# First x turned by TensorE instead of by DMA, w2 loaded earlier, later gelu' of one chunk and a rearranged end in a convolution-and-joint kernel with its gradients

## The chip, the cores and the metric

The kernel runs on one core of a Trainium2 chip. The metric is the time of one execution on the device in microseconds (us); "before" is the median of three runs. A core has TensorE (PE, with its weight loads PEld), VectorE (DVE), ScalarE (ACT), GpSimd (POOL) and SyncE (SP), each with its own queue of instructions in a fixed order. SP here only issues DMA transfers.

## What is computed

A small speech model's forward pass and all of its gradients. x has 2 x 16000 rows of 256 numbers (bfloat16), g has 2 x 8 rows.

```python
h  = gelu(conv3(x, w1))[:, ::2]            # 3 taps, 256x256 each; every second row is kept
f  = gelu(conv3(h, w2))[:, ::2]            # now 2 x 4000 rows
fe = f @ w_f ; ge = g @ w_g
j  = tanh(fe[:, :, None] + ge[:, None])    # 2 x 4000 x 8 x 256
out = j @ w_o
# outputs: out, and the gradients of x, w1, w2, g, w_f, w_g, w_o for a given grad_out
```

## The kernel before

**Chunks.** The 8000 kept positions are cut into 17 chunks: the first has 2 blocks of 128 positions, fifteen have 4 blocks (512 positions), the last has one block of 64. A position needs 4 rows of x. Per chunk there are three stages:

- `stage_a`: XC, the chunk's x with features on the partitions, goes through `conv1` twice (the rows of odd place "o", then those of even place "e"), each followed by `conv_gelu`; then `conv2` and the product with WF, which gives FE. `conv_gelu` (L433 to L490) has per half of the features a Square and a Gelu on ACT (L464, L466) and a product on DVE (L468), then, for the gradient, a tanh on ACT (L476) and five DVE operations (L478 to L486) that write G1o, G1e or G2 ("gelu'"). Its scratch tiles are g_sq (class gsq, three buffers) and g_s (class gs, two buffers); each is opened by the first matmul of a convolution (L460) and held until gelu' is done.
- `stage_j`: in four pairs of the 8 rows of g. JT = tanh(FE + GE) on ACT (L637); for the first two chunks JT is turned by PE and copied to JR (L655), later JR is computed by itself (L660, L665). PE makes the output (L314, WO), the gradient of w_o in GWO, and grad_out times WOT; DVE multiplies it by JT squared (JSQ) into ZS, NGZ and NGP (L705, L720), and the last sum is GN.
- `stage_de`: the way back. GN gives GF, GH and the gradient of x (GX_SB), and with the rows HR, GNR, GHR and XR the gradients of the weights, added up in ACCF, ACC2 and ACC1 (L784) and stored from STAGE at the end (L775). GNR and GHR come by DMA transpose, in the last chunk by PE (`pe_rows`, L745). The gradient of g comes last from NGP by way of NGGE and ngb (L986, L989).

**Memory.** PSUM has seven free banks and one fixed, GWO, into which all chunks add the gradient of w_o.

**The order.** `Flow` takes every operation with its engines, a planned cost and a due time (`F.now` or `at`), and plays a list schedule in which each engine takes the earliest operation that could start, ties by due time. What comes out is the fixed order of every engine's queue. Some evictions (`evac`) may go to ACT or DVE, and the planner chooses. Among its numbers, COLD is the planned moment until which PE is taken as 1.8 times slower, and `land` is how long after its transfer a DMA is taken to arrive.

**The start.** PE runs 28 matmuls on a zeroed tile (L1026). SP turns chunk 0's x (512 KB) on the way by DMA transpose (L338), then the first half of chunk 1's x, then loads w2 (L1040), then the second half. ACT's queue loads w1, POOL's g, w_g, w_f and w_o. The transposed weights W1T, W2T, WG, WFT and WOT are made by PE and an eviction (`turn`, L1046) when the planner finds room.

**The end.** `last_w1` (L959) puts the last two chunks' terms for each tap of w1's gradient into one PSUM bank and stores it; `store` (L976) brings GWO and the others out.

Of the kernel before, what the change touches and what calls it, by code (L numbers as in the profile page):

```python
# [35 lines left out]
class Flow:  # L36
# [4 lines left out]
    TURN = {"TT": 250.0, "TL": 750.0, "SL": 900.0, "LL": 200.0, "TS": 250.0, "LS": 250.0, "SS": 400.0}  # L41
    BACKLOG = {"T": 1450.0, "L": 4500.0, "S": 4500.0}
    NEAR = 300.0
    COLD = 14000.0
    CROWD = 10000.0
    KIND = 16.0

# [162 lines left out]
def kernel(  # L210
# [148 lines left out]

    def load_xc(g_, at, apart=0.0):
        c = chunks[g_]
        XC = st[g_]["XC"] = buf("xr" if c.first else "xc", [P, 17, KT, P], BF16, "XC")
        lo, hi = (1 if c.first else 0), 4 * c.nb + 1
        cuts = ((0, 9), (9, 17)) if g_ == 1 else ((lo, hi),)
        for n_, (b0, b1) in enumerate(cuts):
            dma("SP", lambda b0=b0, b1=b1: XC[:, b0:b1, :, :c.np].rearrange("p j k n -> p (j k) n"),
                lambda b0=b0, b1=b1: dram(xf, 4 * c.q0 - 1 + b0, 4 * c.nb, b1 - b0, c.np),
                r=[], w=[(XC, ("m", n_))], bytes_=(b1 - b0) * c.np * D * 2, new=[XC] if n_ == 0 else [], transpose=True, at=at + n_ * apart,  # L370
                land=2500.0 if c.first else 4500.0)
        if c.first:
            pool_zero(lambda: XC[:, 0, :, 0:1], [], [(XC, "z")], at=at)
            pool_copy(lambda: XC[:, 0, :, 1:P], lambda: XC[:, 4 * c.nb, :, 0:P - 1], 254, [(XC, ("m", 0))], [(XC, "h")], at=at)
        elif c.mid:
            pool_zero(lambda: XC[:, 0, :, c.pb:c.pb + 1], [], [(XC, ("m", 0))], at=at)

    got_op = {}
# [54 lines left out]
    def conv_gelu(g_, jobs, rd, h_buf, pre, ho, gname, gcls, gshape, gsave, news):  # L433

        c = chunks[g_]
        nb, n_ = c.nb, c.np
        W = c.W
        G = buf(gcls, gshape, BF16, gname)
        here = gname == "G2"
        if here:  # L440
            sq, s = buf("gsq", [P, NB, KT, P], BF16, "g_sq"), G
            so, scr = 0, [sq, G]
        elif c.first:
            sq = s = buf("gs" if gname == "G1e" else "gsq", [P, NB, KT, P], BF16, "g_sq")
            so, scr = nb, [sq]
        else:
            sq = buf("gsq", [P, NB, KT, P], BF16, "g_sq")
            s = buf("gs", [P, NB, KT, P], BF16, "g_s")
            so, scr = 0, [sq, s]
        sk = lambda mt: (s, ("s", mt))  # L450
        qk = lambda mt: (sq, ("q", mt))
        both = lambda f: [f(mt) for mt in range(KT)]
        pss = [psum() for _ in range(KT)]
        parts = [(mt, h) for h in range(len(rd)) for mt in range(KT)]
        for k_, (mt, h) in enumerate(parts):
            lst, cost = jobs(mt, h)
            def mms(e, mt=mt, lst=lst):
                for o_, wt, rhs, s_, e_ in lst:
                    mm(o_(pss[mt]), wt(), rhs(), s_, e_)
            op("PE", cost, mms, r=rd[h] + [(sq, "b")], w=[(pss[mt], h)],  # L460
               new=([pss[mt]] if h == 0 else []) + (scr + news if k_ == 0 else []))
        for mt in range(KT):
            ps = pss[mt]
            op("ACT", c_act(W, True), lambda e, mt=mt, ps=ps: nc.scalar.activation(  # L464
                out=sq[:, 0:nb, mt, :n_], in_=blk(ps, c), func=ACT.Square, scale=GELU_SQRT_K), r=[ps], w=[qk(mt)])
            op("ACT", c_act(W, True), lambda e, mt=mt, ps=ps: nc.scalar.activation(  # L466
                out=h_buf[:, ho:ho + nb, mt, :n_], in_=blk(ps, c), func=ACT.Gelu_apprx_tanh), r=[ps], w=[(h_buf, (pre, mt))])
            op("DVE", c_dve(W), lambda e, mt=mt, ps=ps: nc.vector.scalar_tensor_tensor(  # L468
                out=s[:, so:so + nb, mt, :n_], in0=sq[:, 0:nb, mt, :n_], scalar=1.0, in1=blk(ps, c), op0=ALU.add, op1=ALU.mult),
               r=[qk(mt), ps], w=[sk(mt)])  # L470
        k = GELU_A / 2
        N = KT * W
        late = F.now + CW * 0.25
        go_ = 1 if gsave else 0
        full = lambda T_, o_=0: T_[:, o_:o_ + nb, :, :n_]
        op("ACT", c_act(N), lambda e: nc.scalar.activation(out=full(s, so), in_=full(s, so), func=ACT.Tanh, scale=k),  # L476
           r=both(sk), w=both(sk), at=late)
        op("DVE", c_dve(N, 0.25), lambda e: nc.vector.tensor_scalar(  # L478
            out=full(sq), in0=full(sq), scalar1=3.0 * k, scalar2=k, op0=ALU.mult, op1=ALU.add), r=both(qk), w=both(qk), at=late)
        op("DVE", c_dve(N, 0.5), lambda e: nc.vector.tensor_tensor(  # L480
            out=full(sq), in0=full(sq), in1=full(h_buf, ho), op=ALU.mult), r=both(qk) + [(h_buf, (pre, 0)), (h_buf, (pre, 1))], w=both(qk), at=late)
        op("DVE", c_dve(N, 0.25), lambda e: nc.vector.tensor_scalar(
            out=full(sq), in0=full(sq), scalar1=-0.5, scalar2=None, op0=ALU.add), r=both(qk), w=both(qk), at=late)
        op("DVE", c_dve(N, 0.25), lambda e: nc.vector.tensor_scalar(
            out=full(s, so), in0=full(s, so), scalar1=-1.0, scalar2=1.0, op0=ALU.mult, op1=ALU.add), r=both(sk), w=both(sk), at=late)
        op("DVE", c_dve(N, 0.5), lambda e: nc.vector.tensor_tensor(  # L486
            out=full(G, go_), in0=full(s, so), in1=full(sq), op=ALU.mult), r=both(sk) + both(qk), w=[(G, ("g", 0)), (G, ("g", 1))] + (both(sk) if here else []), new=[] if here else [G], at=late)
        st[g_][gname] = G
        if gsave:
            F.now = late  # L490
            halo(g_, G, "g", gname, gsave)
# [16 lines left out]
    def stage_a(g_, t0, dt):  # L508
# [9 lines left out]
        def conv1(l0):  # L518
# [9 lines left out]
                                    i == 0 and kt == 0, i == KK - 1 and kt == KT - 1))  # L528
                return lst, c_pe([m_ * n_] * 6)
            return jobs  # L530
        xm = [(XC, ("m", 0)), (XC, ("m", 1))]
        F.now = t0
        conv_gelu(g_, conv1(2), [xm[:1] + [W1], xm + [W1]] if two else [xm + [W1]], HT, "o", 1, "G1o", "g1o", [P, NB + 1, KT, P], "hg1", [HT])
        F.now = t0 + 0.05 * dt
        halo(g_, HT, "o", "HTo", "hho")
        if c.mid:
            pool_zero(lambda: HT[:, 0, :, c.pb:c.pb + 1], [], [(HT, ("o", "h"))])
        F.now = t0 + 0.12 * dt
        conv_gelu(g_, conv1(0), [xm[:1] + [W1], xm + [W1]] if two else [[XC, W1]], HT, "e", oE, "G1e", "g1e", [P, NB, KT, P], None, [])
        pad_tail(g_, HT, "o", (0, nb + 1))  # L540
        pad_tail(g_, HT, "e", (oE, oE + nb))
        F.now = t0 + 0.3 * dt
# [216 lines left out]
    def grad_rows(g_, name, cls, SRC, nblk, m):  # L759
        if chunks[g_].last:  # L760
            return pe_rows(g_, name, cls, SRC, 1, nblk, m)
        return tile_rows(g_, name, cls, SRC, nblk, lo=1, shape=[P, 2 * NB + (cls == "ghr"), D], land=8000.0)

    def stage():
        stage_n[0] += 1
# [2 lines left out]

    stage_n = [0]

    def acc_add(ACC, key, acc_ap, ps, g_, out, final):
        if final:
            t_ = stage()
            flat = lambda: t_[:, 0:512]
            op("DVE", c_dve(512), lambda e: nc.vector.scalar_tensor_tensor(  # L775
                out=flat(), in0=acc_ap().rearrange("p k d -> p (k d)"), scalar=-1.0, in1=ps[:],
                op0=ALU.mult, op1=ALU.subtract),
               r=[(ACC, key), ps], w=[t_], new=[t_])
            dma("SP", lambda: out.rearrange("(dt p) n -> p dt n", p=P),
# [177 lines left out]
        return terms  # L957

    def last_w1(i):  # L959
        ps = psum()  # L960
        two = [w1_terms(g_, i) for g_ in (LAST - 1, LAST)]
        n = [0, KT * sum(len(t_) for t_ in two)]

        def mms(e, terms):
            for d2 in range(KT):
                for lhs, rhs, _ in terms:
                    mm(ps[:, d2 * D:(d2 + 1) * D], lhs(d2), rhs(), n[0] == 0, n[0] == n[1] - 1)
                    n[0] += 1
        for k, t_ in enumerate(two):
            rd = []  # L970
            for _, _, l in t_:
                rd += [b for b in l if b not in rd]
            op("PE", c_pe([D] * (KT * len(t_))), lambda e, t_=t_: mms(e, t_), r=rd, w=[ps], new=[ps] if k == 0 else [])
        acc_add(ACC1, i, lambda: ACC1[:, i], ps, LAST, out_2[i], True)

    def store(dst, src, r, scale=None, after=()):  # L976
        t_ = stage()
# [44 lines left out]
       r=[(warm, 0)], w=[(warm, 1)])  # L1022
    wps = psum()

    def warm_up(e):
        for _ in range(28):  # L1026
            mm(wps[:, 0:2 * P], warm[:, 0, 0:P], warm[:, 0, 0:2 * P], True, True)
    op("PE", 28 * 120.0, warm_up, r=[(warm, 0)], w=[wps], new=[wps])

    def wload(q, dst, key, out, in_, at, land):  # L1030
        return dma(q, out, in_, r=[], w=[(dst, key)], bytes_=131072, at=at, land=land)

    load_xc(0, BIG)
    op("POOL", 500.0, lambda e: make_identity(nc, ident[:]), w=[ident])
    for i in range(KK):
        wload("ACT", W1, i, lambda i=i: W1[:, i], lambda i=i: w1[i].rearrange("(kt p) n -> p kt n", p=P), BIG, 4000.0)
    for b in range(B):
        dma("POOL", lambda b=b: GR8[:, b, :], lambda b=b: g[b], r=[], w=[(GR8, b)], bytes_=4096, at=BIG + 1, land=5000.0)
    load_xc(1, BIG, 60.0)
    dma("SP", lambda: W2[:].rearrange("p i k n -> p (i k) n"), lambda: w2.rearrange("i (kt p) n -> p (i kt) n", p=P),  # L1040
        r=[], w=[(W2, i) for i in range(KK)], bytes_=393216, load=True, at=BIG + 30.0, land=2500.0)
    wload("POOL", WG, 0, lambda: WG[:], lambda: w_g.rearrange("(kt p) n -> p kt n", p=P), BIG + 1, 8500.0)
    wload("POOL", WF, 0, lambda: WF[:], lambda: w_f.rearrange("(kt p) n -> p kt n", p=P), BIG + 2, 9000.0)
    wload("POOL", WO, 0, lambda: WO[:], lambda: w_o.rearrange("(kt p) n -> p kt n", p=P), BIG + 2, 9000.0)
# [49 lines left out]
    for k in range(NG + 1):  # L1094
# [22 lines left out]
            gg_out(int(k == LAST))  # L1117
        if k == LAST:
            gwg_out()
            store(out_7, lambda: GWO[:], [], after=gwo_ops)  # L1120
    F.now = 1e9
    ctx.enter_context(tc.manual_schedule())
    F.issue()
# [30 lines left out]
```

## Time and profile before

| | us |
|---|---|
| median of three runs | 783.84 (782.11 to 785.67) |
| the profiled execution | 784.01 |
| its span (first to last thing that the profile shows) | 782.1 |
| PE busy | 768.3 |
| DVE busy | 716.1 |
| ACT busy | 716.4 |
| POOL busy | 86.1 |
| first convolution on PE | starts at 8.03 |
| last matmul | ends at 778.0 |

The profile comes from one execution. Times in its views count from the span's start. A row of a timeline has its start, its length, engine, line, operation, written and read tile, shapes, the number of instructions put together, and in brackets how long the engine sat idle before it and what ended that. A row of waits has the waiting engine and line, what it waited for, the sum in us, how often, and the longest. A row of the windows table has the stretch, its length, and for each engine the busy time and the number of instructions, then PE's granted clock (1.00 is full), the DMA engines' share and GB/s. Lines of the kernel after are some 20 higher than those of before.

### The profile page before, as it was taken

The page shows a single profiled execution, that of the slowest core. Times are in us where ns is not written, and L with a number is a line of the kernel's source. Part 1 is how long each engine was busy: PE and PEld are TensorE (multiplying, and loading weights), DVE is VectorE, ACT ScalarE, POOL GpSimd, SP SyncE. Part 2 cuts the span into 40 slices and gives each one's busy share as a digit, 9 for nine tenths or more (in the row PEclk, how much of TensorE's full clock was granted, in tenths as well). Part 3 has the DMA queues.
Part 4 walks back from the last instruction along what each step waited for, and adds up shares of the span by engine and source line. Part 5 has one row for each costly group of instructions (what it writes and reads, how often), then busy time and mean ns, then how long its engine had stood idle before and what let it go on. Part 6 is the DMA issues. An engine that isn't in the chain of part 4 may idle for free.

```text
span 782.1 us, 15385 instructions
## 1 busy us (share of the span) xinstructions
PE 768.3 (98%) x5620; PEld 533.3 (68%) x5620; DVE 716.1 (92%) x1502; ACT 716.4 (92%) x1148; POOL 86.1 (11%) x225
## 2 busy tenths in 40 slices
PE   9799999999999999999999999999999999999997
PEld 7577667576676766767577675766767667677755
DVE  4979999998999999999999999989999999999874
ACT  5999999998999999999999999899999999999761
POOL 3001010201102010020100102001020110201000
PEclk9989999999999999999999999999999999999999
DMA  9999999999999999999999999999999999899672
GB/s 198 232 231 212 233 233 258 239 219 276 216 275 223 232 283 218 252 238 240 272 231 282 230 245 255 237 296 215 275 251 241 233 237 284 175 228 256 172 199 77
DMA packets 394890, 183.82 MB, mean 235 GB/s; under 512 B 320180, under 2 KB 388062, under 8 KB 392894
## 3 DMA queue, kind: packets, MB, share of 16 engines
q1 hardware_dynamic: 393758, 182.03, 100.6%
q8 instruction: 44, 0.72, 0.4%
q0 software_dynamic: 240, 0.41, 0.3%
q10 hardware_dynamic: 816, 0.39, 0.2%
q14 instruction: 32, 0.26, 0.1%
HBM read 52.47 MB, written 50.35 MB: 131 GB/s over the span
## 4 chain that ended last, share of the span: by engine, by line
PE 91%; ACT 4%; DVE 3%; DMA 2%; issue 1%; DVEq 0%; ACTq 0%
PE ps L314 76%; PE GWO L314 13%; DMA GNR<-GN 2%; PE psb L583 1%; DVE g_s L468 1%; ACT JT L637 1%; ACT JSQ L696 1%; PE psb L655 1%; ACT g_sq L464 1%; ACT HT L466 0%; DVE NGZ L705 0%; ACT JR L665 0%; DVE GH L846 0%; ACT JR L323 0%; PE psb L1055 0%
## 5 line engine op out<-in xcount | busy, mean ns | idle before, releaser
L637 ACT ACTIVATE JT<-FE,GE 128x512 bf16<-128x512 bf16 (+4 forms) x288 | 179.7, 686 | 0.3 <-DVE FE L328 0.2
L705 DVE SCALAR_TENSOR_TENSOR NGZ<-JSQ,ps 128x512 f32<-128x512 bf16 (+3 forms) x252 | 151.2, 608 | 7.2 <-PE ps L314 5.5
L314 PE MATMUL ps<-WO,JT 128*128 128x256 bf16 (+1 forms) x1008 | 151.8, 274 | 0.0
L314 PE MATMUL ps<-GOT,WOT 128*128 128x512 bf16 (+2 forms) x544 | 151.2, 364 | 0.1
L696 ACT ACTIVATE JSQ<-JT 128x1024 bf16<-128x1024 bf16 (+2 forms) x130 | 132.4, 1018 | 10.5 <-DVE NGZ L705 7.8
L314 PEld LDWEIGHTS <-JT 128*128 128x128 bf16 (+1 forms) x1008 | 98.8, 98 | 60.1
L323 ACT CAST OUT_SB<-ps 128x512 bf16<-128x512 f32 (+1 forms) x203 | 121.4, 606 | 15.2 <-PE ps L314 14.9
L314 PE MATMUL GWO<-GO_R,JR 128*128 128x256 bf16 (+1 forms) x1008 | 131.2, 273 | 0.3 <-ACT JR L323 0.3
L665 ACT ACTIVATE JR<-JR 128x1024 bf16<-128x1024 bf16 (+1 forms) x116 | 122.9, 1065 | 7.9 <-DVE JR L660 7.9
L720 DVE TENSOR_TENSOR ZS<-ZS,NGZ 128x1024 f32<-128x1024 f32 (+2 forms) x102 | 115.3, 1131 | 0.7
L314 PEld LDWEIGHTS <-JR 128*128 128x128 bf16 (+1 forms) x1008 | 98.2, 98 | 15.3 <-ACT JR L323 0.6
L314 PEld LDWEIGHTS <-W 128*128 128x128 bf16 x636 | 60.0, 98 | 60.1 <-issue 1.1
L314 PE MATMUL ps<-W1T,GH 128*128 128x256 bf16 (+2 forms) x506 | 94.2, 325 | 0.0
L314 PE MATMUL ps<-XC,W 128*128 128x512 bf16 (+2 forms) x432 | 86.5, 351 | 0.0
L314 PE MATMUL ps<-GHR,XR 128*128 128x256 bf16 (+1 forms) x756 | 85.6, 273 | 0.7 <-ACT GHR L323 0.7
L314 PEld LDWEIGHTS <-XR 128*128 128x128 bf16 (+1 forms) x756 | 73.8, 98 | 9.4 <-issue 0.8
L660 DVE TENSOR_TENSOR JR<-FER,GEB 128x1024 bf16<-128x1024 bf16 (+1 forms) x116 | 77.8, 673 | 0.0
L784 DVE TENSOR_TENSOR ACC<-ACC,ps 128x512 f32<-128x512 f32 x87 | 57.6, 679 | 16.1 <-PE ps L314 16.0
L314 PEld LDWEIGHTS <-WOT 128*128 128x128 bf16 x544 | 51.3, 99 | 29.7 <-issue 1.7
L314 PEld LDWEIGHTS <-GH 128*128 128x128 bf16 (+1 forms) x506 | 49.3, 98 | 24.6 <-issue 0.2
L325 ACT ACTIVATE GX_SB<-ps 128x512 bf16<-128x512 f32 (+1 forms) x88 | 52.5, 619 | 10.1 <-PE ps L314 9.7
L314 PE MATMUL ps<-GNR,HR 128*128 128x256 bf16 (+1 forms) x504 | 59.5, 273 | 1.3 <-DMA GNR<-GN 1.3
(130 smaller groups left out, 981.7 us busy)
## 6 DMA issues: line engine op xcount, KB each, us to landing
GO_R<-in_grad_out_dram SPq DMA_DIRECT2D x60, 512.0 KB, 5.3
out_dram<-OUT_SB SPq DMA_DIRECT2D x60, 512.0 KB, 4.8
XR<-in_x_dram SPq DMA_DIRECT2D x15, 1088.0 KB, 8.0
out_dram<-GX_SB SPq DMA_DIRECT2D x30, 512.0 KB, 3.4
out_dram<-STAGE SPq DMA_DIRECT2D x9, 128.0 KB, 3.5
GOT<-GO_R SPq DMA_TRANSPOSE x68, 6.2
GO_R<-in_grad_out_dram SPq DMA_DIRECT2D x4, 256.0 KB, 3.5
out_dram<-OUT_SB SPq DMA_DIRECT2D x4, 256.0 KB, 4.9
```

The lines of the kernel that those rows point to most:

```text
L314: nc.tensor.matmul(ps_ap, lhsT=lhsT, rhs=rhs, start=start, stop=stop)
L323: nc.scalar.copy(out=dst(), in_=src())
L325: nc.scalar.activation(out=dst(), in_=src(), func=ACT.Copy, scale=scale)
L464: op("ACT", c_act(W, True), lambda e, mt=mt, ps=ps: nc.scalar.activation(out=sq[:, 0:nb, mt, :n_], in_=blk(ps, c), func=ACT.Square, scale= ...
L468: op("DVE", c_dve(W), lambda e, mt=mt, ps=ps: nc.vector.scalar_tensor_tensor(out=s[:, so:so + nb, mt, :n_], in0=sq[:, 0:nb, mt, :n_], scal ...
L637: op("ACT", c_act((hi - lo) * nb, ptr=True), lambda e, j=j, mt=mt, lo=lo, hi=hi, b=b: nc.scalar.activation(out=cut(JT[:, j, mt, :W], lo, h ...
L660: op("DVE", c_dve(na * 2 * D, 0.5), lambda e, h=h, na=na, JR=JR: nc.vector.tensor_tensor(out=JR[:n_, 0:na], in0=S["FER"][:n_, 2 * h:2 * h ...
L665: op("ACT", c_act(na * 2 * D), lambda e, na=na, JR=JR: nc.scalar.activation(out=JR[:n_, 0:na], in_=JR[:n_, 0:na], func=ACT.Tanh), r=[JR], ...
L696: nc.scalar.activation(out=JSQ[:, :, :W], in_=JT[:, j, :, :W], func=ACT.Square)
L705: nc.vector.scalar_tensor_tensor(out=cut(Z[:, d2, :W], lo, hi), in0=cut(JSQ[:, d2, :W], lo, hi), scalar=1.0, in1=cut(ps[:, :W], lo, hi), o ...
L720: nc.vector.tensor_tensor(out=o_, in0=i0, in1=i1, op=ALU.add)
L784: op("DVE", c_dve(512), lambda e: nc.vector.tensor_tensor(out=acc_ap().rearrange("p k d -> p (k d)"), in0=acc_ap().rearrange("p k d -> p ( ...
```

## The change

Chunk 0's x comes in rows (two plain loads into XL), is turned by PE in 16 transposes, and four evictions write XC. w2 is first in SP's queue. The identity that PE's transposes need is made first on POOL. The warm-up has 20 matmuls instead of 28. The gelu' of chunk 1 is due 0.8 of a chunk after its place instead of 0.25. GNR and GHR of the chunk before the last are planned to land sooner, and the last chunks' terms of tap 0 of w1's gradient are summed in GWO's bank, after GWO has been stored, instead of in a free bank.

```diff
-    COLD = 14000.0
+    COLD = 7000.0
...
+    def rows_xc(c, XC, at):
+
+        XL = buf("out", [P, 4 * c.nb, D], BF16, "XL")
+        for h in range(2):
+            src = xf[0:8 * P, :].rearrange("(p r) d -> p r d", r=8)[:, 4 * h:4 * h + 4, :]
+            dma("SP", lambda h=h: XL[:, 4 * h:4 * h + 4, :], lambda src=src: src, r=[], w=[(XL, h)], bytes_=P * 2048,
+                new=[XL] if h == 0 else [], load=True, at=at, land=2000.0)
+        pool_zero(lambda: XC[:, 0, :, 0:1], [], [(XC, "z")], new=[XC], at=at)
+        for h in range(2):
+            ps = psum(BF16)
+
+            def trs(e, h=h, ps=ps):
+                for n in range(8):
+                    nc.tensor.transpose(out=ps[:, n * P:(n + 1) * P], in_=XL[:, 4 * h + n // 2, n % 2 * P:(n % 2 + 1) * P],
+                                        identity=ident[:])
+            op("PE", c_pe([P] * 8), trs, r=[(XL, h), ident], w=[ps], new=[ps], at=at)
+            for k in range(2):
+                evac(lambda h=h, k=k: XC[:, 1 + 4 * h + 2 * k:3 + 4 * h + 2 * k].rearrange("p j k n -> p (j k n)"),
+                     lambda k=k, ps=ps: ps[:, k * 512:(k + 1) * 512], 512, r=[ps], w=[(XC, ("m", 2 * h + k))], f=0.5, at=at)
+        pool_copy(lambda: XC[:, 0, :, 1:P], lambda: XC[:, 4 * c.nb, :, 0:P - 1], 254, [(XC, ("m", 3))], [(XC, "h")], at=at)
+
...
-        late = F.now + CW * 0.25
+        late = F.now + CW * (0.8 if g_ == 1 else 0.25)
...
-        return tile_rows(g_, name, cls, SRC, nblk, lo=1, shape=[P, 2 * NB + (cls == "ghr"), D], land=8000.0)
+        return tile_rows(g_, name, cls, SRC, nblk, lo=1, shape=[P, 2 * NB + (cls == "ghr"), D],
+                         land=3000.0 if g_ == LAST - 1 else 8000.0)
...
     def last_w1(i):
-        ps = psum()
+        ps = GWO if i == 0 else psum()
+        pv = GWO.t[:].rearrange("p k v -> p (k v)") if i == 0 else None
...
+    WARM = 20
+
     def warm_up(e):
-        for _ in range(28):
+        for _ in range(WARM):
             mm(wps[:, 0:2 * P], warm[:, 0, 0:P], warm[:, 0, 0:2 * P], True, True)
...
+    op("POOL", 800.0, lambda e: make_identity(nc, ident[:]), w=[ident])
     load_xc(0, BIG)
-    op("POOL", 500.0, lambda e: make_identity(nc, ident[:]), w=[ident])
...
     dma("SP", lambda: W2[:].rearrange("p i k n -> p (i k) n"), lambda: w2.rearrange("i (kt p) n -> p (i kt) n", p=P),
-        r=[], w=[(W2, i) for i in range(KK)], bytes_=393216, load=True, at=BIG + 30.0, land=2500.0)
+        r=[], w=[(W2, i) for i in range(KK)], bytes_=393216, load=True, at=BIG - 1.0, land=2500.0)
...
-            store(out_7, lambda: GWO[:], [], after=gwo_ops)
+            store(out_7, lambda: GWO[:], [GWO], after=gwo_ops)
```

## The prediction

> **What bounds the kernel now.** I read the page first: busy shares, then the slices.
>
> ```profile
> PE 768.3 (98%) x5620; PEld 533.3 (68%) x5620; DVE 716.1 (92%) x1502; ACT 716.4 (92%) x1148; POOL 86.1 (11%) x225
> ...
> PE   9799999999999999999999999999999999999997
> ...
> PEclk9989999999999999999999999999999999999999
> ```
>
> TensorE (PE) is busy for 768.3 of 782.1 us. Only the first and last slices are not full, and in the third the granted clock falls to 0.8. So the time is PE's fixed work plus what PE loses at both ends. The waits of PE over the whole span say where:
>
> ```profile
> PE psb L655 <- ACT JT L637: 3.7, 3, 1.9
> PE ps L314 <- DMA GNR<-GN: 1.3, 2, 1.0
> PE ps L314 <- DVE ngb L989: 1.2, 1, 1.2
> PE ps L314 <- DVE g_sq L1020: 1.1, 1, 1.1
> PE ps L314 <- ACT GHR L323: 0.7, 1, 0.7
> PE ps L314 <- DVE JR L328: 0.6, 1, 0.6
> ```
>
> The largest, 3.7 us, lies at 34.7 to 39.2: PE must turn chunk 0's tanh tiles JT, and ScalarE (ACT) is late with them. The windows table there (columns after the length: busy PE, PEld, DVE, ACT, POOL; then the granted clock):
>
> ```profile
> 34.00:36.00 2.00, 0.91 (x9) 0.61 (x7) 2.00 (x5) 2.00 (x5) 0.00 (x0) 1.00 1.18 201
> 36.00:38.00 2.00, 0.23 (x1) 0.10 (x1) 1.97 (x5) 2.00 (x5) 0.91 (x3) 0.86 1.18 324
> 38.00:40.00 2.00, 1.13 (x8) 0.89 (x9) 1.41 (x5) 2.00 (x5) 0.00 (x0) 0.50 1.17 336
> 40.00:42.00 2.00, 2.00 (x11) 1.39 (x10) 1.84 (x5) 1.87 (x3) 0.00 (x0) 0.50 1.21 249
> ```
>
> ACT and VectorE (DVE) are full while PE starves, and the starved PE is granted half its clock until about 44.2. From 39.16 to 44.2 PE runs 5 + 8 transposes, 16 matmuls of 256 columns and the first few of a GWO group in 5.0 us; by the full-clock steps of the same forms (0.056 and 0.109) they need 2.6. So this place costs 3.7 + 2.4 us. ACT's timeline shows what stands ahead of the missing tiles:
>
> ```profile
> 31.77 1.06 ACT L476 ACTIVATE g_s<-g_s 128x1024 bf16<-128x1024 bf16 x1
> ...
> 36.62 1.08 ACT L476 ACTIVATE g_s<-g_s 128x1024 bf16<-128x1024 bf16 x1
> 37.57 2.14 ACT L637 ACTIVATE JT<-FE,GE 128x256 bf16<-128x256 bf16 x4
> ```
>
> Those are tanhs of chunk 1's gelu', which nobody needs before chunk 1's backward stage. At the start two rows of PE's timeline matter:
>
> ```profile
> 8.03 2.78 PE L314 MATMUL ps<-XC,W 128*128 128x256 bf16 x24
> ...
> 12.98 1.48 PE L314 MATMUL ps<-HT,W 128*128 128x256 bf16 x12 [0.20 <-DMA W<-in_w_dram]
> ```
>
> The first convolution starts at 8.03; the second one waits a little for w2. At the end:
>
> ```profile
> 762.34 0.38 PE L314 MATMUL ps<-WG,ngb 128*8 128x256 bf16 x2 [1.22 <-DVE ngb L989]
> ...
> 776.53 1.47 PE L314 MATMUL ps<-GHR,XR 65*128 65x256 bf16 x12 [0.67 <-ACT GHR L323]
> ```
>
> **The built order.** After PE's 1,497th matmul (about 205 us by the counts of the windows) the orders of before and after agree on PE for 3,958 matmuls, up to the last 20 us. So only the first 205 us and the tail can differ in kind.
>
> **Start, up to chunk 0's second convolution.** Removed: one DMA transpose of 512 KB and 8 warm-up matmuls (0.21 us each, twice the 0.109 that the same form takes later, though the clock's column says 1.00 there). Added: two plain loads of 256 KB, 16 PE transposes (0.056 each at full clock: 0.9 us), 4 evictions of 128x512 bf16 (the W1T ones take 0.59 on ACT, 0.42 on DVE). SP issues w2 (384 KB), the two loads, then both halves of chunk 1's x. In before w1's and x's 0.9 MB moved between 2.0 and 6.1 us at 0.25 MB per us on average. Now w1, w2 and the first x are 1.28 MB: at that rate, and at most 0.29 (the 512-byte and 256-byte rows after 12 us), they are in at 6.4 to 7.1 us, and up to 7.5 if half of the 0.38 MB of POOL's weight loads goes between. I take 7.3. PE's queue is 20 warm-ups (to 5.3), 12 transposes of w2 (landed by about 5 us), 8 of x, 12 of w1 with 8 of x between: never empty. The last x transposes end near 8.1; 0.2 to the eviction, which queues behind a W1T copy on ACT and ends near 8.9. First convolution at 8.9, **0.9 later**. ACT then runs its 8 Square/Gelu in six plus tanh plus two, without the 0.49 wait in front of the tanh, and the second convolution has w2 long since: 0.6 of the 0.9 comes back. Term: **+0.25 us** on what follows; bounds -0.5 (data in at 6.4) to +3.0 (below).
>
> *A page's rule.* The Trainium skill, "TensorE: Matmul & The Clock Gate", Part 4, says that PE-mode transposes do not count as PE-busy for the clock gate, and Part 1 there gives a busy window of about 3.4 us. The trace has 5.9 us of half-clock warm-ups and then full clock, and no long run of transposes in a cold clock, so no row settles it.
>
> **Filling, 20 to 50 us.** The w2 transposes and evictions (12 at 0.056, 3 at 0.34 us on DVE) and WG's go from the full stretch to the idle start. Chunk 1's three tanhs go behind the tiles: in ACT's new order all 16 JT tiles of chunk 0 stand ahead of the first; by the steps of the timeline (12 Square and Gelu at 0.48, 11 JT 128x256 at 0.40, JR 0.9, two JSQ at 0.53, OUT 0.46) the work from 19.7 to the last of them is 12.6 us: ready at 32.3 instead of 39.6. That wait goes. What is late next? PE alone: from chunk 1's convolution at 16.28 to chunk 2's at 50.28 are 34.0 us, less 4.6 idle, less 2.4 of clock, less 0.9 moved away: 26.1, so PE could be there at 42.7. But chunk 2's convolution opens a g_s buffer, there are two, and both are held by chunk 1's gelu' until DVE has written G1o and G1e. DVE in the new order, from its first chunk 1 row (20.55 + 0.25): 6 at 0.60 (L468), 7 OUT at 0.60, 5 JR at 0.60, 7 ZS/GN sums at 0.60, 16 NGZ/ZS halves at 0.34, and 13 gelu', FE and JSQ pieces for 5.7 us until G1o is written: 26.1 us. So not before 46.9: **3.4 ahead** of 50.28; G1e follows 2.9 later, 3.9 ahead of before's 53.73. ACT, counted the same way (17.9 us more), gets to chunk 2's first Square at 50.3 instead of 52.22, with three JT tiles (0.61 each) more and one tanh (0.95) fewer done: 2.8 ahead. From 60 to 90 us all three engines were full (PE 30.00, DVE 29.90, ACT 29.95 of 30), so PE keeps no more than these two bring. Term, including the late start: **-3.2 us**. Bounds: 0 (PE starves elsewhere for as long) and -6.5 (3.7 + 2.4 + the waits of 0.6 and 0.3 at JR, less 0.5).
>
> **End.** The ngb wait of 1.2 us goes: sixteen GHR matmuls (1.74 us) stand there now, in GWO's bank that the store at 760.94 has freed. GNR, issued at 750.3 and 4.3 to landing in that stretch, is used near 758; a late one costs what it is late. The GHR wait of 0.7 goes: the gradient rows come ahead of the W1T products (1.3 us). But those products, their evictions and the GX store now end last: SP issues them (0.6 + 0.35) just ahead of the last three stores (0.52 each); the last issue ends about 2.0 us after PE's last matmul, where it was 1.45. Term 1.2 + 0.7 - 0.6, rounded: **-1.2 us**; bounds 0 and -1.9.
>
> The numbers of the planner (COLD, the landing times, the warm-up's cost) run nowhere on the chip; what they do is in the orders counted above.
>
> **Sum.** The profiled execution took 784.01 us (span 782.1; 1.9 around it), 0.2 over the median 783.84. 784.0 - 3.2 - 1.2 = **779.6 us**, 0.56% less. About 0.5% (3.9 us) is what a measurement here tells from no change, so faster means under 780.1: the forecast sits on the line.
>
> **Rivals.**
> - *The whole loss goes* (0.12). PE does other work until the buffers free, and ACT and DVE make up the rest in their 5% of slack after 100 us: 784.0 - 6.0 - 1.5 = 776.5. For: that slack. Against: 60 to 90.
> - *A wait takes the place of the one removed* (0.18): PE idles in one piece ahead of chunk 2's convolution (46.9 against 42.7 is up to 4.2 us), and the clock halves once more, as it did after 34.7, for 2.4 us. 779.6 + 2.4 = 782.0.
> - *Transposes keep the clock down* (0.12): after 4.3 us of warm-ups the 28 transposes do not bring full clock. They take 0.107 each, the convolution starts at 9.8 and its 24 matmuls take 5.1 us; chunk 0's second convolution is 3.0 late instead of 0.25: 779.6 + 2.8 = 782.4. For: the shorter warm-up. This is what the Trainium skill's rule on transposes would do. Against: 28 warm-ups in a row were granted nothing before 6.9 either, so it may be time alone.
> - *Slower than before* (0.08): the clock stays at half through the whole of chunk 0's and 1's first stages, to about 22 us. PE has some 14 us of full-clock work in 8 to 22, so it costs 7: 786.6. It decides once half clock lasts over 9 us of PE work. Against: at 39.2 a busy PE had its clock back after 5 us.
> - *It doesn't do what it says*: not so; the orders show each move.
>
> **How the numbers follow.** Forecast 0.50 (778 to 781.2; two thirds of it under 780.1). Faster 0.33 + 0.12 = 0.45; same 0.17 + 0.18 + 0.10 (most of the third rival) = 0.45; slower 0.02 + 0.08 = 0.10. The range takes in the bounds of the terms up to the third rival with its own spread, and leaves out the slow one: 776.0 to 784.0.
>
> **What would show it.** Right: no JT wait of PE in 30 to 42; the first convolution near 8.9 at 0.109 us a matmul; chunk 2's convolution near 47 with a wait for DVE's G1o ahead of it; no ngb and GHR waits. Wrong: convolutions of 0.213 us a matmul after 9 us; granted clock under 1 between 40 and 55; chunk 2's convolution later than 49 or earlier than 45; waits for GNR in the tail.

## The result, and the profile after

Twenty runs of each kernel: after 781.51 us (median; 779.31 to 783.75), before 785.28 (782.11 to 788.52). The ratio is 0.9947, 95% interval 0.9935 to 0.9958: 0.5% faster, where 0.56% was forecast. As a time it is further off: 779.6 was forecast, counted from a before of 784.0, and before itself came out at 785.28 in these twenty. In a later session, on the chip of the last four experiments, the ratio was 0.9976 (0.9961 to 0.999), with 781.51 against 783.7. Single executions of one kernel spread over 4 to 6 us, and the two that were profiled lie at opposite ends: before's 784.01 would be among the fastest five of its twenty, after's 783.46 is among the slowest three. So these two traces differ by 0.4 us of span (782.1 and 781.7), and where the medians' difference comes from can't be read off this pair alone. A second trace of each kernel, taken for that, helps below.

PE's busy time and the slices of the page of after:

```profile
PE 767.7 (98%) x5628; PEld 532.3 (68%) x5628; DVE 718.5 (92%) x1509; ACT 713.2 (91%) x1145; POOL 81.2 (10%) x225
...
PE   7999989999999999999999999999999999999997
...
PEclk9999999999999999999999999999999999999999
```

The dip of the clock in the third slice is gone. The first slice is emptier (7), the second, 7 in before, is full, and a new hole stands in the sixth (8 where before had 9). PE's waits in after say what they are:

```profile
PE GWO L314 <- ACT JR L684: 2.4, 1, 2.4
PE psb L1090 <- DMA GR<-in_g_dram: 1.4, 1, 1.4
...
PE ps L314 <- DVE XC L328: 0.8, 1, 0.8
PE psb L1078 <- DMA W<-in_w_dram: 0.7, 1, 0.7
...
PE psb L674 <- ACT JT L656: 0.3, 1, 0.3
```

The waits for JT (3.7), GNR (1.3), ngb (1.2) and GHR (0.7) are 0.3, 0, 0 and 0. New are waits at the start (0.7 for w2, 1.4 for g's rows, 0.8 for the first x in XC), and one of 2.4 for JR near 98 us. The windows where before starved, in after:

```profile
36.00:38.00 2.00, 2.00 (x22) 1.76 (x20) 2.00 (x5) 2.00 (x4) 0.00 (x0) 1.00 0.92 272
38.00:40.00 2.00, 1.60 (x19) 1.23 (x17) 2.00 (x6) 2.00 (x5) 0.00 (x0) 1.00 1.26 244
```

PE has 2.00 and 1.60 of 2 us here at full clock; before had 0.23 and 1.13, at 0.86 and 0.50.

**A ledger.** Four points are easy to find in every timeline of PE: M0, the first matmul of chunk 0's second convolution; M1, the start of chunk 2's first convolution; M2, the second half of chunk 5's first-layer convolution (a row of 12 matmuls of 512 columns, at 188.79 in before), from about which on the built orders agree up to the tail; M3, the first W1T product near 755. Differences between them, in us:

| | to M0 | M0 to M2 | M2 to M3 | M3 to last matmul's end | from there to the end | span |
|---|---|---|---|---|---|---|
| before | 12.98 | 175.81 | 566.02 | 23.19 | 4.1 | 782.1 |
| before, second trace | 13.25 | 175.78 | 565.62 | 23.19 | 4.2 | 782.0 |
| after | 16.33 | 174.92 | 564.76 | 21.23 | 4.5 | 781.7 |
| after, second trace | 14.94 | 172.41 | 564.78 | 21.23 | 4.4 | 777.8 |

The first pair: +3.35 - 0.89 - 1.26 - 1.96 + 0.36 = -0.4. The second pair, both from one chip: +1.69 - 3.37 - 0.84 - 1.96 + 0.28 = -4.2. The end is worth the same in both. It reads, in after's timeline of PE:

```profile
775.76 0.60 PE L314 MATMUL GWO<-GHR,XR 65*128 65x256 bf16 x4
776.20 1.04 PE L314 MATMUL ps<-GHR,XR 65*128 65x256 bf16 x8
```

without a bracket, where before waited for GHR. The two traces of after differ in two places, the start (1.4) and M0 to M2 (2.5), and in no other.

**The start of after** in its first trace, PE's timeline:

```profile
5.48 0.84 PE L1078 MATMUL psb<-ident,W 128*128 128x128 bf16 x12 [0.67 <-DMA W<-in_w_dram]
...
8.40 0.20 PE L1090 MATMUL psb<-ident,GR 8*128 8x8 bf16 x2 [1.41 <-DMA GR<-in_g_dram]
...
10.62 4.61 PE L314 MATMUL ps<-XC,W 128*128 128x256 bf16 x24 [0.80 <-DVE XC L328]
...
16.33 1.47 PE L314 MATMUL ps<-HT,W 128*128 128x256 bf16 x12
```

and in its second trace:

```profile
8.32 0.20 PE L1090 MATMUL psb<-ident,GR 8*128 8x8 bf16 x2 [1.00 <-DMA GR<-in_g_dram]
...
10.54 0.39 PE L314 MATMUL ps<-XC,W 128*128 128x256 bf16 x2 [0.80 <-DVE XC L328]
11.15 2.56 PE L314 MATMUL ps<-XC,W 128*128 128x256 bf16 x22 [0.22 <-ACT XC L323]
```

Both wait until 8.3 to 8.4 us for the second of g's two 4 KB loads, whose transposes stand in PE's queue ahead of all of w1's and of half of x's. After the longer waits (0.67, 1.41, 0.80) the 24 matmuls take 4.61 us, with granted clock 0.50 between 11 and 14; in the second trace they take 2.95. The last section shows what decided between the two.

**The hole near 98 us.** SP in before, then SP, DVE and PE in after's first trace:

```profile
80.42 0.42 SPq L340 DMA_DIRECT2D GEB<-GED  x1
...
91.01 0.57 SPq L340 DMA_DIRECT2D GEB<-GED  x1
...
97.86 1.90 DVE L679 TENSOR_TENSOR JR<-FER,GEB 128x1024 bf16<-128x1024 bf16 x3 [2.73 <-DMA GEB<-GED]
99.70 1.89 PE L314 MATMUL GWO<-GO_R,JR 128*128 128x256 bf16 x8 [2.43 <-ACT JR L684]
```

and the clock behind it:

```profile
100.00:102.00 2.00, 2.00 (x10) 1.26 (x9) 1.97 (x6) 2.00 (x5) 0.00 (x0) 0.50 1.21 239
102.00:104.00 2.00, 2.00 (x9) 0.79 (x7) 1.48 (x3) 0.88 (x3) 0.80 (x3) 0.76 1.08 245
```

GEB is the table of g's part that DVE adds to FE before JR. Before issued it at 80.42 us, 7 us ahead of its use at 87.6, and nobody waited. After issues it at 91.01: in SP's new order it stands behind the DMA transposes of GOT (82.23) and HR (86.18), which in before came after it, and behind a store of OUT_SB that waits 0.3 us for its data. It lands at 97.8. DVE, then ACT, then PE wait, and PE, idle for 2.4 us, comes back at half clock: 8 GWO matmuls take 1.89 us instead of 1.04, and by the two windows some 1.5 us go. In the second trace GEB is issued at 89.16, PE waits 1.6 us and keeps its clock. Those 2.4 + 1.5 against 1.6 are 2.3 of the 2.5 us by which the two traces differ there.

### The profile page after: what moved, and what is told of

The parts are those of the page before. It is cut to its first block, busy times and chain, and to the rows that moved or that the text cites. A ratio compares the mean times of both kernels' runs of the same rounds, so it can differ in the third digit from the quotient of the medians.

```text
span 781.7 us, 15397 instructions
## 1 busy us (share of the span) xinstructions
PE 767.7 (98%) x5628; PEld 532.3 (68%) x5628; DVE 718.5 (92%) x1509; ACT 713.2 (91%) x1145; POOL 81.2 (10%) x225
## 4 chain that ended last, share of the span: by engine, by line
PE 84%; ACT 8%; DVE 4%; DMA 2%; issue 1%; POOL 0%; DVEq 0%; SPq 0%; ACTq 0%; POOLq 0%
PE ps L314 71%; PE GWO L314 13%; ACT JT L656 2%; ACT JSQ L715 1%; ACT OUT_SB L323 1%; DMA GEB<-GED 1%; PE psb L602 1%; DMA XR<-in_x_dram 1%; DMA GR<-in_g_dram 1%; ACT HT L485 1%; ACT g_sq L483 1%; ACT JR L684 1%; DVE g_s L487 0%; DVE NGZ L724 0%; DVE ZS L739 0%
## 5 line engine op out<-in xcount | busy, mean ns | idle before, releaser
L314 PE MATMUL ps<-WO,JT 128*128 128x256 bf16 (+1 forms) x1008 | 150.0, 273 | 0.1
L323 ACT CAST OUT_SB<-ps 128x512 bf16<-128x512 f32 (+1 forms) x198 | 118.2, 606 | 13.1 <-PE ps L314 12.9
L314 PE MATMUL ps<-XC,W 128*128 128x512 bf16 (+2 forms) x432 | 89.1, 358 | 0.9 <-DVE XC L328 0.8
L314 PE MATMUL ps<-GHR,XR 128*128 128x256 bf16 (+1 forms) x736 | 83.3, 273 | 0.0
L483 ACT ACTIVATE g_sq<-ps 128x512 bf16<-128x512 f32 (+2 forms) x102 | 57.2, 562 | 3.2 <-PE ps L314 3.2
```

The lines of the kernel that those rows point to most:

```text
L314: nc.tensor.matmul(ps_ap, lhsT=lhsT, rhs=rhs, start=start, stop=stop)
L323: nc.scalar.copy(out=dst(), in_=src())
```

## The experiments

Those that went to a chip together share it; e1 to e4 ran on one, f1 to f4 on a second, g1 to g4 on a third. The kernel before had medians of 785.6, 785.2 and 783.7 us there, and ratios are to these.

**The three parts by themselves.** First the start alone in the kernel before (`rows_xc`, w2, the identity, warm-up, COLD):

```diff
-    COLD = 14000.0
+    COLD = 7000.0
...
-        r=[], w=[(W2, i) for i in range(KK)], bytes_=393216, load=True, at=BIG + 30.0, land=2500.0)
+        r=[], w=[(W2, i) for i in range(KK)], bytes_=393216, load=True, at=BIG - 1.0, land=2500.0)
```

> The kernel before with the start alone: x in rows, w2 first, 20 warm-ups, the planner's COLD. Theory A (three separate gains, and the start costs): the profiled execution of the changed kernel had chunk 0's second convolution at 16.33 instead of 12.98, so by itself the start is a loss that the room left by the moved w2 transposes (0.9 us of PE, 1.5 of DVE) only partly pays back: 1 to 2.5 us slower than before, ratio 1.001 to 1.003. Theory B (the start is what gains, the rest is noise of the plan): 2 to 4 us faster, ratio 0.995 to 0.9975.

Measured: 784.71, ratio 0.9991 (0.9976 to 1.0007): nothing that can be told from no change, so neither theory's time came. M0 lies at 15.81; M0 to M2 takes 175.23, 0.6 less, about the net 0.7 us of w2, WG and WO transposes that changed sides of M0. The waits for JT stay (3.4).

Then the later gelu' alone:

```diff
-        late = F.now + CW * 0.25
+        late = F.now + CW * (0.8 if g_ == 1 else 0.25)
```

> The kernel before with chunk 1's gelu' later, and nothing else. Theory A: the wait of PE for JT tiles (3.7 us) and the half clock after it (2.4 us) go, and DVE and ACT give back some: 2.5 to 4.5 us faster, ratio 0.994 to 0.997; no JT wait over 1 us between 30 and 45 us, granted clock 1.00 there. Theory B: the w2 evictions still stand in DVE's full stretch, the same time is lost in another wait: within 1 us of before.

Measured: 783.26, ratio 0.9973 (0.9953 to 0.9992), near theory A's range, but without its signs: of the waits for JT 2.1 us remain, and the wait for JR, which before does not have, is there with 2.1 and half a clock behind it (12 convolution matmuls in 4.09 us instead of 2.75; GEB is issued at 92.13 here): M0 to M2 is 177.39 in this trace, 1.6 longer than before's. So the hole near 98 us comes from the later gelu' and not from the start.

Then the end alone:

```diff
-        return tile_rows(g_, name, cls, SRC, nblk, lo=1, shape=[P, 2 * NB + (cls == "ghr"), D], land=8000.0)
+        return tile_rows(g_, name, cls, SRC, nblk, lo=1, shape=[P, 2 * NB + (cls == "ghr"), D],
+                         land=3000.0 if g_ == LAST - 1 else 8000.0)
...
-        ps = psum()
+        ps = GWO if i == 0 else psum()
```

> The kernel before with the end alone (landing time of the chunk before the last, first tap's terms in GWO's bank). Theory A: the waits for ngb (1.2) and GHR (0.7) go, the last stores are 0.3 to 0.6 later: 1.2 to 1.7 us faster, ratio 0.998 to 0.9985. Theory B: the stores behind the last matmul grow by what PE gains: within 0.5 us of before.

Measured: 782.97, ratio 0.9967 (0.9952 to 0.9983). M3 to the last matmul is 21.23 as in after, 1.96 less than before, and 0.4 longer from there to the end: a gain of 1.6 that stands by itself, as theory A has it (the median gained more, 2.6).

**g's rows out of the way.** After, with g's two loads on ACT's queue ahead of w1:

```diff
-        dma("POOL", lambda b=b: GR8[:, b, :], lambda b=b: g[b], r=[], w=[(GR8, b)], bytes_=4096, at=BIG + 1, land=5000.0)
+        dma("ACT", lambda b=b: GR8[:, b, :], lambda b=b: g[b], r=[], w=[(GR8, b)], bytes_=4096, at=BIG - 2.0, land=5000.0)
```

> The changed kernel with the two 4 KB loads of g issued first on ACT's queue instead of on POOL's behind the identity, so that PE's transposes of g don't wait in front of w1's and x's. PE runs the same warm-ups and transposes. Theory A (gaps in PE's work took the clock: 0.67 for w2, 1.41 for g, 0.80 for XC): the g wait goes, the first convolution starts near 9.5 and runs at 0.109 us a matmul, 2 to 3 us faster than the changed kernel's profiled execution, 5 to 7 us faster than before, ratio 0.991 to 0.994. Theory C (PE transposes don't count for the clock gate): the convolution starts 1 us earlier but still at 0.213 us a matmul until 3 to 4 us later; 1 us gained at most, ratio 0.9935 to 0.9945.

Measured: 791.39, ratio 1.0069 (1.0051 to 1.0088), the opposite of a cure. PE's timeline:

```profile
10.03 0.61 PE L1078 MATMUL psb<-ident,W 128*128 128x128 bf16 x4 [3.02 <-DMA W<-in_w_dram]
...
14.68 0.61 PE L1078 MATMUL psb<-ident,W 128*128 128x128 bf16 x4 [2.98 <-DMA W<-in_w_dram]
...
16.81 5.31 PE L314 MATMUL ps<-XC,W 128*128 128x256 bf16 x24 [0.67 <-ACT XC L323]
```

w1's three taps were issued at 1.76, 2.22 and 2.74 us instead of 0.74, 1.35 and 1.87, and the last one landed at 14.7: 0.9 us of delay (0.4 in the expectation of the next run is too little) becomes 6 us of waiting. Chunk 1's two DMA transposes are under way on SP meanwhile (2.3 to 15.6 us in after), and that they hold up what is left on the other queues would explain both this and g's late landing. No run isolates it: POOL's weight loads also went 1.2 us sooner here, though in the next kernel they do so too and w1 is in time.

So the next one puts g on SP's queue, between the x loads and chunk 1's DMA transposes:

```diff
-        dma("POOL", lambda b=b: GR8[:, b, :], lambda b=b: g[b], r=[], w=[(GR8, b)], bytes_=4096, at=BIG + 1, land=5000.0)
+        dma("SP", lambda b=b: GR8[:, b, :], lambda b=b: g[b], r=[], w=[(GR8, b)], bytes_=4096, load=True, at=BIG, land=5000.0)
```

> The changed kernel with the two 4 KB loads of g in SP's own queue, behind the two loads of x and ahead of chunk 1's DMA transposes, so that nothing of w1, w2 or x moves later. Theory D (once SP's DMA transposes run, packets of the other queues crawl: in the run with g on ACT's queue w1's last tap landed at 14.7 us because it was issued 0.4 us later, and in the changed kernel g landed at 8.3 for the same reason): g is in by 7.5, PE's wait for it falls from 1.4 to under 0.4, the first convolution starts at 9.3 to 9.8, 1 us faster than the changed kernel, or 3 if the clock is then kept; ratio to before 0.991 to 0.9935. Theory E (the start's lateness is hidden by ACT and DVE later): as the changed kernel, 0.994 to 0.9955.

Measured: 779.58, ratio 0.9923 (0.9906 to 0.994).

```profile
8.73 0.39 PE L314 MATMUL ps<-XC,W 128*128 128x256 bf16 x2 [0.19 <-DVE XC L328]
9.34 2.56 PE L314 MATMUL ps<-XC,W 128*128 128x256 bf16 x22 [0.22 <-ACT XC L323]
...
13.67 1.47 PE L314 MATMUL ps<-HT,W 128*128 128x256 bf16 x12
```

The convolution starts at 8.73 at full clock and M0 is at 13.67. The wait for g is gone, but more than g's place changed. PE now turns g behind the convolution (11.84), and SP's DMA transposes moved. SP in after, then here:

```profile
2.29 13.27 SPq L338 DMA_TRANSPOSE XC<-in_x_dram  x2
...
4.81 6.82 SPq L338 DMA_TRANSPOSE XC<-in_x_dram  x2
```

The first of them waited here 1.8 us for a weight load to land; issued 2.5 us later, both were through 3.9 us sooner, and POOL's three weight loads landed 6.0 to 6.5 us after their issue instead of 10.0 to 11.9. How much of the start's gain is due to g and how much to this isn't shown. GEB is issued at 87.59 here, and PE no longer waits for JR (DVE still waits 1.7 us for GEB): M0 to M2 is 171.68.

**GEB half a chunk sooner.** After, with the load of chunk 2's GEB due earlier:

```diff
-                r=[GED], w=[(GEB, 2 * h), (GEB, 2 * h + 1)], bytes_=(hi - lo) * 2048, load=True, at=at(2 * h + 1),
-                behind=[got_op[c.i - 1, 1]])
+                r=[GED], w=[(GEB, 2 * h), (GEB, 2 * h + 1)], bytes_=(hi - lo) * 2048, load=True, at=at(2 * h + 1) - (0.5 * CW if c.i == NTR else 0.0),
+                behind=[got_op[c.i - 1, 0 if c.i == NTR else 1]])
```

> The changed kernel with the rows of ge for chunk 2 (GEB) loaded half a chunk sooner: the first of its two loads is issued near 56 us instead of 91, the second is planned half a chunk sooner. Theory F (the chunk 1 to chunk 2 passage took back 2.4 us of what the later gelu' gave: PE waited for JR, JR for GEB, whose load stood in SP's queue behind a store that waited): the 2.4 us wait of GWO for ACT's JR goes, 1.5 to 2.5 us faster than the changed kernel, ratio to before 0.9915 to 0.993. Theory G (ACT and DVE were behind there anyway): the wait is for another operation of ACT or DVE, within 0.7 us of the changed kernel.

Measured: 779.76, ratio 0.9937 (0.9918 to 0.9955). The gain is smaller than theory F's. The wait for JR is gone, M0 to M2 is 170.88, but this came in its place, between 200 and 260 us:

```profile
PE ps L314 <- DMA GNR<-GN: 2.8, 2, 1.7
```

M2 to M3 is 567.87 instead of 564.8. Such a wait for the DMA transpose GNR, near 250 us, is in before (1.0 and 0.7 there in its two traces) and in the start alone (2.6), and in neither trace of after: the end alone has it too (1.4). What decides whether it comes isn't shown.

**Both.** The edits of the last two kernels together:

> The changed kernel with both: g by SP ahead of the DMA transposes, GEB for chunk 2 sooner. Theories D and F: the two gains add, 3 to 4.5 us faster than the changed kernel, ratio to before 0.989 to 0.991. Theories E and G: no faster than the better of the two alone.

Measured: 778.24, ratio 0.9914 (0.9897 to 0.993). It is the fastest of all: 0.9% under before, and by the ratio, which was taken on another chip, also under after. M0 13.41, M0 to M2 171.26, M2 to M3 564.93. SP's transposes start at 4.67 here as well. Its interval overlaps that of g on SP's queue alone, so what GEB adds to it isn't settled.

**Do transposes bring the clock up?** The kernel before, its 28 warm-up matmuls replaced by 54 transposes (and the identity made ahead of them):

```diff
-        for _ in range(28):
-            mm(wps[:, 0:2 * P], warm[:, 0, 0:P], warm[:, 0, 0:2 * P], True, True)
+        for _ in range(54):
+            nc.tensor.transpose(out=wps[:, 0:P], in_=warm[:, 0, 0:P], identity=ident[:])
```

> The kernel before with its 28 warm-up matmuls replaced by 54 transposes of a zero tile against the identity, about as long (5.7 us at half clock). It tells only about PE's clock in the first 15 us. Theory C (transposes don't count for the clock gate): they take 0.107 us each to the end, and so do w1's transposes behind them; the first convolution runs at 0.213 us a matmul for 3 us or more. Theory A (any work of PE counts): w1's transposes and the convolution run at 0.056 and 0.109 as in the kernel before, if PE isn't left waiting over 1 us in front of it.

Measured (one execution): 784.12.

```profile
1.36 5.88 PE L1028 MATMUL psb<-ident,g_sq 128*128 128x128 bf16 x54 [1.36 <-POOL XC L352]
...
8.23 2.78 PE L314 MATMUL ps<-XC,W 128*128 128x256 bf16 x24
```

The transposes run at 0.109 us each, twice the 0.056 of full clock, and the convolution behind them takes the 2.78 us that it takes in before: with nothing but transposes ahead, the clock came up. The Trainium skill, "TensorE: Matmul & The Clock Gate", Part 4, says of transpose mode that it doesn't count as PE-busy in the same way; this trace does not agree, if its transposes, which it records as MATMUL, ran in that mode. The prediction's other reading, that time alone brings the clock up, has no run with an idle PE at its start; later in a run time alone was not enough (g on ACT's queue: 13.65 us at half clock, in whose first 6.8 us PE worked for 2.0).

**What w2's place does.** The kernel before with w2's load first on SP, nothing else:

```diff
-        r=[], w=[(W2, i) for i in range(KK)], bytes_=393216, load=True, at=BIG + 30.0, land=2500.0)
+        r=[], w=[(W2, i) for i in range(KK)], bytes_=393216, load=True, at=BIG - 1.0, land=2500.0)
```

> The kernel before with one edit of the change's start alone: w2's load stands first in SP's queue instead of behind the first half of chunk 1's DMA transposes. The first x still comes by DMA transpose. Theory H (the place of w2 is what makes the start of before uneven: its second convolution began at 12.98, 15.06, 15.38 and 15.82 us in four traces with the same start): no wait for w2 ahead of chunk 0's second convolution, but the 384 KB go ahead of the first x, so the first convolution starts about 1.3 us later (near 9.3 instead of 8.03); the second convolution near 14.2, the whole 0.5 to 2 us faster than before by medians. Rival (the first x's transfer is what counts, w2 costs only what it displaces): the first convolution is 1.3 to 2.5 us later and the whole 0 to 1.5 us slower.

Measured: 783.82, ratio 1.0006 (0.9993 to 1.0019). The wait for w2 is gone, but the first convolution starts at 10.22 and M0 is at 15.02. Theory H falls; the rival holds, at its lower end: M0 to M2 is 174.30, 1.5 shorter, and pays for the 1.8 by which M0 is later.

**The change without the later gelu'** (after, with one line put back):

```diff
-        late = F.now + CW * (0.8 if g_ == 1 else 0.25)
+        late = F.now + CW * 0.25
```

> The kernel after without the later gelu' of chunk 1: start and end of the change together. Theory I (the later gelu' needs the new start to work, and the end's gain adds up by itself): the waits for JT come back with 3 us or more, chunk 2's convolution starts 36.6 us or more behind chunk 0's second one (before 37.3, the start alone 36.6, after 35.1), and the time is the sum of the start alone (-0.9 us) and the end alone (-2.6): ratio near 0.996. Rival (the start frees PE, DVE and ACT of the w2 work by itself, and the gelu' is only a part): the distance is 35 to 36 us and the ratio at or under 0.995.

Measured: 783.35, ratio 0.9989 (0.9974 to 1.0004). The waits for JT are back (3.4), M0 to M1 is 36.56 and M0 to M2 175.15, so the mechanism is as theory I has it: without the later gelu' the filling gains only the moved 0.7. The ratio is nearer to 1 than its 0.996; that on this chip the start costs more than on the first (M0 at 15.10 against 13.25) fits, but isn't shown to be the reason.

**Both kernels once more.** No edit.

> The kernel after, unchanged, for a second trace of it. If its first trace was a slow one of its spread (783.46 us where the median was 781.51): chunk 0's second convolution starts about 0.5 to 1.5 us sooner than 16.33, with a shorter wait for g's rows or at full clock, the rest from there as in the first trace (739.7 us to the first W1T product near 755, 21.2 from there to the last matmul). The rival, that the difference arises all over the run: the start as before to 0.3 us and another distance in the middle. Ratio near 0.995 again.

> The kernel before, unchanged, for a second trace of it. If its first trace was a fast one of its spread: chunk 0's second convolution starts between 14 and 16 us instead of 12.98, with a longer wait for w2, as in the three kernels that have the same start; the distance from there to the first W1T product near 755 is 741.8 us to 0.5. Rival: the same start and a longer middle.

Measured: after 781.51, ratio 0.9976 (0.9961 to 0.999); the profiled execution took 779.64, the fastest of its twelve. M0 is 1.4 sooner as expected, but M0 to M3 is 737.19 and not 739.7: the wait for JR was shorter and kept its clock, which the expectation had left out. Before: 783.85, M0 at 13.25. The expectation (14 to 16) was wrong, and with it the idea that 12.98 was a lucky draw of one and the same spread. The three kernels with before's start whose M0 is at 15.06 to 15.82 ran on the other two chips, where SP's third DMA transpose, issued right behind w2, took 6.4 to 7.1 us; in the two traces of before itself it took 5.3 and 5.0. That may be the chip (that of before's first trace isn't on record); five traces don't show more.

## Why the prediction held, step by step

The total came out as forecast (0.9947 against 0.9944) in the first session, and at under half of it in the last. Its steps did worse than its sum, and that the sum came out is in good part luck. By the second pair of traces, which add up to -4.2 us where -4.4 was forecast, start and filling together brought -1.7 where -3.2 was forecast (that figure held the late start already), the end -1.7 where -1.2 was, and -0.8 came from a stretch that the forecast left out. By the first pair start and filling even cost 2.5. The median, 781.51, lies in the stated range (776.0 to 784.0) but just above the 778 to 781.2 that the forecast itself stood for.

Of the prediction's own signs, two of being right were there: no JT wait to speak of, no ngb and GHR waits. Two were not: the first convolution was at 10.6 and 10.5 and not near 8.9, and chunk 2's convolution, at 51.40 and 49.89, had no wait for G1o ahead of it. That is also its sign of being wrong "later than 49", and the slow convolution after 9 us in the first trace is another.

*Start, +0.25 us.* Measured on one chip +1.7, between the two first traces +3.35; by kernels with the one and the other start on the first and second chips (15.81 against 15.38 and 15.82; 15.47 against 15.06) 0 to +0.4. The step that failed is "never empty": the list of PE's queue left out the four small transposes of g, whose load came last and landed at 8.3 us. With g on SP's queue the convolution started at 8.73, where 8.9 was forecast, and M0 was at 13.67, 0.4 over the forecast 13.23; but there SP's transposes went later too, so this doesn't show that the rest of the step was sized right, and the rate of the first loads was not (last section). The bound of +3.0 was for transposes in a cold clock; in the first trace the convolution did run at half clock and M0 was 3.35 late, close to it, but what took the clock was idle time.

*Filling, -3.2 us.* (The prediction read the first and last slices of PE as the ones not full; on its page they are the second, 7, and the last.) The diagnosis held: the JT wait went from 3.7 to 0.3, and with it the half clock. Its size was worked out with a marker that moved. "Chunk 2's convolution not before 46.9, 3.4 ahead" gave 51.40 and 49.89, near before's 50.28. G1o, which it was to wait for, is written 0.5 us ahead of it in both; PE's own work with some small waits set it, and the 26.1 us put down for that work left out what the new order added. Adding up PE's matmuls in the built orders from M0 to M1 by their full-clock steps (0.056, 0.109 and 0.216 us) gives 28.4 us in before and 31.24 in after: the same 16 W and WG transposes fewer, but 16 transposes of JT, 16 products with WO, 8 GWO and 4 transposes of WO more. Time less work is what was lost:

| | M0 to M1 | of it work | lost | M0 to M2 | of it work | lost after M1 |
|---|---|---|---|---|---|---|
| before | 37.30 | 28.4 | 8.9 | 175.81 | 166.5 | 0.4 |
| start and end, no later gelu' | 36.56 | 27.7 | 8.8 | 175.15 | 165.9 | 0.4 |
| after | 35.07 | 31.2 | 3.8 | 174.92 | 165.9 | 5.2 |
| after, second trace | 34.95 | 31.2 | 3.7 | 172.41 | 165.9 | 2.8 |
| after, g on SP and GEB sooner | 34.91 | 31.2 | 3.7 | 171.26 | 165.9 | 1.7 |

So the gain up to M1 was 5.1 us of lost time and 0.7 of moved work, nearer to the rival "the whole loss goes" than to the forecast. Then the new wait for JR took back 1.6, or 3.9 with its clock, and about 1.2 went in small pieces. What is left from M0 to M2 is -0.9 and -3.4, and with the late start +2.5 and -1.7. That GEB's load moves behind two DMA transposes and a store was in SP's built order, and the prediction had not looked at SP's queue between the start and the tail: of the moved step, only ACT's, DVE's and PE's instructions were counted. DVE's count (26.1 us from its first row of chunk 1 to G1o) was good: 27.2 in both traces of after. It began at 23.68 and 22.18 instead of 20.8.

*The rival "a wait takes the place of the one removed"* thus happened, with its halved clock, but 50 us later and for another reason than it named. Its 782.0 is nearer to the median 781.51 than the forecast 779.6 is.

*End, -1.2 us.* Measured -1.6 and -1.7: PE gains 1.96 (1.2 + 0.7 were forecast) and the stores give back 0.3 to 0.4 instead of 0.6. One reading was off: the sixteen GHR matmuls that now stand ahead of ngb write an ordinary bank (765.65); GWO's bank gets its sixteen behind it, at 768.04.

*Not in the sum:* M2 to M3 is 0.8 to 1.3 us shorter, of which 0.7 and 1.0 are the wait for GNR near 250 us that after doesn't meet.

*Transposes keep the clock down* is refuted as it stood: in all traces of kernels with this start the transposes behind the warm-up came to full clock (0.056 us each), and 54 transposes in place of the warm-up did not keep it down. So is the slower rival: from 15 us to 99 the clock was full.

What stays open: which share of the medians' difference (3.8 and 2.2 us) is the chip's and which that of chance at the wait for JR; a single trace of a kernel shows one execution. The medians of the three parts alone add up to -5.8 us, but each is known to 1.2 to 1.5 us either way, so this doesn't show that they fail to add up.

## What to carry to other kernels

Before you price a moved block by when some later instruction starts, add up the work that the new order puts ahead of it, and follow the block's small loads through the DMA queues' own order too: here a table of 256 KB behind two DMA transposes took back 1.6 to 3.9 of the 5.8 us that the rearrangement had gained. A load that is needed early belongs well ahead of the first long DMA transpose, whatever its size: with 4 KB of g issued 0.1 us ahead of it, PE waited until 8.3 us. And trace both kernels twice before you read a difference of half a per cent out of two traces.

## What the runs showed of the hardware

- Plain loads in the first microseconds of after moved 349 and 357 GB/s (3.75 to 6.5 us, two traces) where 250 to 290 were reckoned with; with chunk 1's DMA transposes under way all queues together moved 93 to 154 GB/s (7 to 15 us, in windows of 2 us). In before, whose third transpose ran from 7.3 to 12.6 us, they moved 155 to 290 between 8 and 15, so a transpose under way doesn't by itself mean a low rate.
- PE's granted clock changes only at the ends of windows of 3.41 us that follow one another without a gap. Inside the runs every stretch at half clock lasts 3.41, 6.83 or 13.65 us, and the two of after's first trace begin 88.75 us apart, which is 26 windows. Rows cut at such windows, two of after's first trace (10.78 to 14.20 is the half clock) and two of its second, PE's busy time first:

```profile
7.37:10.78 3.41, 1.58 (x24) 1.38 (x25) 1.76 (x7) 0.86 (x3) 0.00 (x0) 1.00 1.23 130
10.78:14.20 3.42, 3.30 (x17) 2.16 (x16) 0.54 (x2) 1.70 (x5) 0.39 (x1) 0.50 1.13 108
...
6.56:9.97 3.41, 2.19 (x35) 1.79 (x32) 1.66 (x6) 1.60 (x3) 0.00 (x0) 1.00 1.07 134
9.97:13.39 3.42, 2.63 (x23) 2.22 (x24) 1.52 (x5) 2.19 (x7) 0.62 (x3) 1.00 1.33 127
```

- In the first trace the waits for g and for XC fall into one window, in the second into two. In the fourteen traces, before their last 10 us, PE lost its clock behind every window in which it was busy for 1.6 us or less (15 of them); at 1.8 us it kept it three times and lost it once; with more it never lost it. It got it back behind windows with 2.75 us of work or more. So a wait of 1.81 us (start alone) cost the clock and one of 1.74 (without the later gelu') did not, and of the waits for JR those of 2.4 and 2.1 did and the one of 1.6 did not. Where the windows lie differs from execution to execution: full clock first came between 3.8 and 7.1 us. The Trainium skill, "TensorE: Matmul & The Clock Gate", Part 1, says that the window in which activity is judged is about 3.4 us long and free-running; these traces agree with both.
